# A decode-step backward kernel: the store of one 1280 KB weight-gradient block moved from Pool's DMA queue to ScalarE's, cut into 124 and 4 partitions

## The chip, the cores and the metric

One core of a Trainium2 chip. The metric is the device time of one execution in microseconds; the kernel before takes 739.5 us, the median of 3 runs (739.39 to 740.98).

## What is computed

The forward step and all gradients of a block that adds an attention with a KV cache and a gated MLP to its input, for one token:

```
xn  = layernorm(x)                                    # x: 1 x 640
q   = (xn @ wq)                                       # 32 heads of 128
p_h = softmax(q_h @ K_h^T / sqrt(128))                # K_h, V_h: 8192 x 128 for each head
o_h = p_h @ V_h
out = x + o @ wo + (silu(xn @ w1) * (xn @ w3)) @ w2
gradients of out, weighted with grad_out, by x, K, V, wq (640 x 4096), wo (4096 x 640), w1, w3, w2
```

All tensors are bfloat16. Nearly all of the bytes are K and V, which are read once, and dK and dV, which are written once: 2 MB each for every head. The gradient of wq is an outer product, dwq = xn^T dq, of 5 MB in all.

## The kernel before

The 32 heads run one after the other, in groups of four (`GH = 4`, `g` is the group), and everything is issued in an order that is written out by hand. For each head the four tiles of 128 partitions x 64 positions x 128 are handled like this: `product` multiplies K by q (V by grad_out @ wo^T) on VectorE and adds up over the 128 columns with matmuls by an identity; `probs`, `row_dots` and `dscores` make the softmax and its gradient; `outer` makes dV and dK, 48 of 64 rows on VectorE and 16 on ScalarE (L380, L387).

Transfers are in three queues:

- SP (`nc.sync`) loads K and V: V of head h+2 in the middle of head h (L115), K of head h+3 towards its end (L109). It also stores dV and dK of the last two heads, in halves (L392).
- Pool (`nc.gpsimd`) stores dV and dK of the other heads (L394), 2 MB each.
- ScalarE (`nc.scalar`) loads wo of the next group of heads at the second head of a group (L144) and stores the finished group's gradient of wo (L319). ScalarE takes these DMAs in its own order of instructions, between activations.

Weights of wq come in four blocks of eight heads (1024 columns, `GW = 8`), in two buffers `wq_0` and `wq_1` (`wq_bufs`). The gradient of a block is written over the block itself by ScalarE (L323, five activations for a group), in `finish_steps`, which is a generator: each `gap()` in the loop over the heads runs one step of it. For groups 0 to 5 the block's second group (odd `g`) starts the block's store. Blocks 0 and 1 go out from Pool column by column (L331, L396). Block 2, whose gradient is complete at head 24, and which is in a buffer that nothing loads again, goes into the list `late`; this list is given to Pool at head 29, behind the store of that head's dK (L126). Three stores are in it: wq's block 2 (1280 KB), wo of group 6 (640 KB) and wq of group 6 (640 KB).

`prep_steps(g)` makes q and the gradient of o for the next group. It needs wo of that group: `turn` transposes it on TensorE (L253), ScalarE copies it (L258), and L276 multiplies. TensorE works strictly in the order written, so what stands behind L253 waits with it: at head 26 that is the rest of this head's matmuls.

Of the kernel before, what the change touches and what calls it, by code (L numbers as in the profile page):

```python
# [16 lines left out]
P = 128  # L17
# [4 lines left out]
def kernel(  # L22
# [22 lines left out]
    nc = tc.nc  # L45
# [42 lines left out]
    dwq_v = out_4.rearrange("(p ci) n -> p ci n", ci=NC)  # L88
# [9 lines left out]
    with tc.manual_schedule(engines=ORDERED):  # L98
# [23 lines left out]
        def store(dst, src, later=False):  # L122
            if later:
                late.append((dst, src))
            else:
                nc.gpsimd.dma_start(dst, src)  # L126
# [164 lines left out]
        def on_cols(g):  # L291
            on = small.tile([P, GH], F32, name="on")
            nc.scalar.copy(on[:], grp[g]["on_ps"])
            on_bf = small.tile([P, GH], BF16, name="on_bf")
            nc.scalar.copy(on_bf[:], on[:])
            return on, on_bf
# [8 lines left out]
        def finish_steps(g):  # L305
            G_ = grp[g]
            wo_g = G_["wo"]
            on, on_bf = on_cols(g)
            behind_o.append((g, on_bf))
            yield  # L310
            assert not behind_o
            for r in range(GH):
                nc.scalar.activation(wo_g[:, r, :], g_bc_bf[:], ACTF.Copy, scale=on[:, r:r + 1])
                if r == 1:
                    yield
            if g == NG - 2:
                store(dwo_v[g], wo_g[:], True)
            else:
                nc.scalar.dma_start(dwo_v[g], wo_g[:])  # L319
            yield  # L320
            b, k = divmod(g, HB)
            for ci in range(NC):
                nc.scalar.activation(G_["wq"][:, ci, :], G_["dqbc"][:].rearrange("p h d -> p (h d)"),  # L323
                                     ACTF.Copy, scale=xn_col[:, ci:ci + 1])
            if g < NG - HB and k == HB - 1:
                cols = slice(b * GW * DH, (b + 1) * GW * DH)
                if g == NG - HB - 1:
                    store(dwq_v[:, :, cols], G_["wq_all"][:], True)
                else:
                    columns.extend((dwq_v[:, ci, cols], G_["wq_all"][:, ci, :]) for ci in range(NC))  # L330
                    nc.gpsimd.dma_start(*columns.pop(0))  # L331
            if g >= NG - HB:
                store(dwq_v[:, :, g * GH * DH:(g + 1) * GH * DH], G_["wq"], True)
            grp.pop(g)
# [148 lines left out]
        def keep_dq(st):  # L483
            G_, hh = st.G, st.hh
            if hh == 0:
                G_["dqbc"] = wpool.tile([P, GH, DH], BF16, name="dqbc_g", tag="dqbc_g", bufs=1)
            nc.scalar.copy(G_["dqbc"][:, hh, :], st.ps_db[:])
            if hh == GH - 1 and st.g < NG - 1:
                steps.append(finish_steps(st.g))
# [305 lines left out]
```

## Time and profile before

| | before |
|---|---|
| time, median of 3 runs | 739.5 us |
| the profiled execution: its own time / its span on the chip | 739.76 us / 737.9 us |
| busy: VectorE / TensorE / ScalarE / Pool | 85% / 76% / 63% / 7% of the span |
| DMA | 303.69 MB, mean 412 GB/s |
| DMA queue of SP / Pool / ScalarE | 155.41 MB / 139.42 MB / 7.87 MB |
| granted TensorE clock, mean | 0.774 |
| last VectorE instruction ends | 719.8 us |

Durations come from one profiled execution, and times inside it are counted from the start of its span. Its own time is 1.86 us more than the span, and 0.26 us more than the median of the runs. A DMA is worked on by 16 DMA engines at once, and its landing is the time at which the last of them is done. The line numbers are those of the kernel before; from L329 on the changed kernel's lines are one higher.

### The profile page before, as it was taken

The numbers are of one execution on the slowest core, as the hardware profiler recorded it, in microseconds if no ns is written. First come the engines' busy times: TensorE is split into PE (matmuls) and PEld (weight loads), VectorE is DVE, ScalarE is ACT, GpSimd is POOL, SyncE is SP. The second block draws the span as 40 slices with busy tenths as digits, with TensorE's granted clock in tenths as the row PEclk, the third lists the DMA queues.
The fourth block names the chain that finished last, engine by engine and source line by source line (L and its number), as shares of the span: only waits on it lengthen the run. The fifth ranks groups of instructions, "written<-read, shape, count | busy, mean of one in ns | idle before, by whom it ended". The sixth has DMA issues, their size and how long they took to land.

```text
span 737.9 us, 15773 instructions
## 1 busy us (share of the span) xinstructions
PE 560.1 (76%) x6498; PEld 326.3 (44%) x6513; DVE 628.8 (85%) x708; ACT 467.3 (63%) x1395; POOL 48.6 (7%) x93
## 2 busy tenths in 40 slices
PE   4768888786888788767788877787878767887860
PEld 3554445443544445434444434444444434454440
DVE  3689999997899989877998979699599988999990
ACT  2384566784678666674677656587377846777650
POOL 0010000000000110100000100100000000000100
PEclk9798779767777779667986788688678878867765
DMA  9998999999999999999999999999999999999992
GB/s 332 415 410 311 407 432 428 428 428 429 428 429 429 422 432 426 430 425 427 432 428 426 431 428 425 428 428 426 427 422 410 428 422 432 409 430 430 419 407 106
DMA packets 28389, 303.69 MB, mean 412 GB/s; under 512 B 3116, under 2 KB 4846, under 8 KB 10910
## 3 DMA queue, kind: packets, MB, share of 16 engines
q1 hardware_dynamic: 15202, 155.41, 50.6%
q0 software_dynamic: 11376, 139.42, 44.6%
q10 hardware_dynamic: 1740, 7.87, 2.6%
q8 instruction: 51, 0.84, 0.4%
q14 instruction: 20, 0.16, 0.1%
HBM read 151.34 MB, written 151.34 MB: 410 GB/s over the span
## 4 chain that ended last, share of the span: by engine, by line
DMA 60%; DVE 23%; PE 10%; ACT 3%; issue 1%; SPq 1%; DVEq 0%; ACTq 0%
DMA out_dram<-ot 33%; DMA Kt<-in_A_k_cache_dram 23%; DVE T L365 10%; DVE ot L387 8%; PE psS L367 3%; DMA out_dram<-wo_g 2%; DMA w3t<-in_B_w_dram 2%; ACT ot L380 2%; PE ob L451 1%; PE ob L429 1%; PE psDP L367 1%; DVE DP_sb L436 1%; SPq L158 1%; PE dx_ps L592 1%; DVE S_sb L402 1%
## 5 line engine op out<-in xcount | busy, mean ns | idle before, releaser
L367 PE MATMUL psDP<-T,ident_bf 128*128 128x512 bf16 x512 | 187.7, 533 | 58.0 <-DVE T L365 57.8
L367 PEld LDWEIGHTS <-ident_bf 128*128 128x128 bf16 x1024 | 123.8, 123 | 238.6 <-issue 191.1
L380 ACT ACTIVATE ot<-qs_g,Uf 128x128 bf16<-128x128 bf16 x496 | 151.5, 390 | 60.4 <-DMA out_dram<-ot 18.3
L365 DVE TENSOR_TENSOR T<-Kt,qs_g 128x4096 bf16<-128x4096 bf16 x64 | 146.4, 2289 | 30.6 <-DMA Kt<-in_A_k_cache_dram 29.1
L367 PE MATMUL psS<-T,ident_bf 128*128 128x512 bf16 x512 | 152.2, 451 | 21.6 <-DVE T L365 21.4
L380 ACT ACTIVATE ot<-do_g,Pf 128x128 bf16<-128x128 bf16 x504 | 154.0, 389 | 5.4 <-DMA out_dram<-ot 4.4
L365 DVE TENSOR_TENSOR T<-Vt,do_g 128x4096 bf16<-128x4096 bf16 x64 | 146.1, 2282 | 0.7 <-ACT do_g L284 0.6
L387 DVE TENSOR_TENSOR ot<-qs_g,U 128x3072 bf16<-128x3072 bf16 (+1 forms) x64 | 113.2, 1769 | 23.8 <-DMA out_dram<-ot 23.8
L387 DVE TENSOR_TENSOR ot<-do_g,P 128x3072 bf16<-128x3072 bf16 (+1 forms) x64 | 112.9, 1763 | 5.5 <-DMA out_dram<-ot 4.4
L394 POOL DMA_DIRECT2D out_dram<-ot x60 | 32.1, 535 | 583.0 <-DVE Uf L449 315.9
L451 PEld LDWEIGHTS <-Kt 128*128 128x128 bf16 x2048 | 57.7, 98 | 11.0 <-issue 8.2
L451 PE MATMUL ob<-U,Kt 128*128 128x1 bf16 x2048 | 57.1, 164 | 1.7 <-DVE U L444 1.5
L429 PEld LDWEIGHTS <-Vt 128*128 128x128 bf16 x2048 | 56.8, 98 | 0.0
L429 PE MATMUL ob<-P,Vt 128*128 128x1 bf16 x2048 | 56.1, 163 | 0.0
L423 ACT ACTIVATE Pf<-E,rZ 128x16 f32<-128x16 f32 x32 | 9.7, 305 | 59.8 <-DVE rZ L419 59.8
L470 ACT ACTIVATE dq_diag<-ident_bf,odq 128x128 bf16<-128x128 bf16 x32 | 12.8, 401 | 48.2 <-DVE odq L466 48.2
L406 PE MATMUL sm<-ident_f,mrow 128*128 128x128 f32 x64 | 18.6, 380 | 22.6 <-DVE mrow L404 22.4
L258 ACT COPY woT<-ps_t 128x512 bf16<-128x512 bf16 x40 | 23.0, 577 | 20.0 <-PE ps_t L253 20.0
L440 PE MATMUL sm<-rdot,ones_fc 128*128 128x1 f32 x64 | 11.3, 246 | 21.6 <-DVE junk L439 21.5
L253 PE MATMUL ps_t<-ident_bf,wo_g 128*128 128x128 bf16 x160 | 18.3, 247 | 10.2 <-ACT woT L258 6.7
L440 PEld LDWEIGHTS sm<-rdot,ones_fc 128*128 128x128 f32 x64 | 10.5, 191 | 34.3 <-DVE junk L439 32.2
L402 DVE TENSOR_REDUCE S_sb<-psS 128x64 f32<-128x512 f32 x32 | 21.9, 685 | 3.1 <-PE psS L367 3.1
(154 smaller groups left out, 501.6 us busy)
## 6 DMA issues: line engine op xcount, KB each, us to landing
out_dram<-ot POOLq DMA_DIRECT2D x60, 2048.0 KB, 30.5
Kt<-in_A_k_cache_dram SPq DMA_DIRECT2D x32, 2048.0 KB, 26.7
Vt<-in_A_v_cache_dram SPq DMA_DIRECT2D x32, 2048.0 KB, 21.5
out_dram<-ot SPq DMA_DIRECT2D x8, 1024.0 KB, 16.5
out_dram<-wo_g ACTq DMA_DIRECT2D x6, 640.0 KB, 15.5
wo_g<-in_A_wo_dram ACTq DMA_DIRECT2D x6, 640.0 KB, 15.8
wq<-in_A_wq_dram SPq DMA_DIRECT2D x2, 1280.0 KB, 27.8
out_dram<-wq POOLq DMA_DIRECT2D x10, 256.0 KB, 35.0
```

Source lines behind the costliest of these rows:

```text
L253: nc.tensor.transpose(ps_t[:, hh * DH:(hh + 1) * DH], wo_g[:, hh, ci * P:(ci + 1) * P], ident_bf[:])
L258: nc.scalar.copy(woT[:], ps_t[:])
L365: nc.vector.tensor_tensor(T[:], src[:, :, ds_], vec[:, ds_].unsqueeze(1).to_broadcast([P, J, DHH]), ALU.mult)
L367: nc.tensor.matmul(ps[:], lhsT=ident_bf[:], rhs=T[:, :, RUN * i:RUN * (i + 1)], start=(half == 0 and i == 0), stop=(half == 1 and i == DHH ...
L380: nc.scalar.activation(st.ot[:, j1 - ACT_J + j].rearrange("p a b -> p (a b)"), vec, ACTF.Copy, scale=wf[:, half, j:j + 1])
L387: nc.vector.tensor_tensor(st.ot[:, j0:j1], vec.rearrange("p (a b) -> p a b", b=2).unsqueeze(1).to_broadcast([P, n, DH // 2, 2]), w2[:, j0: ...
L394: nc.gpsimd.dma_start(dst[h], rows)
L402: nc.vector.tensor_reduce(st.S[:], st.ps["S"][:], AX.X, ALU.add)
L406: nc.tensor.matmul(st.sm[:, 8:8 + P], lhsT=mrow[:].to_broadcast([P, P]), rhs=ident_f[:], start=True, stop=True, skip_group_check=True)
L429: nc.tensor.matmul(st.ob[:, 0:1], lhsT=st.V[:, j, :], rhs=st.P2[:, j, 0:1], start=(j == 0), stop=(j == J - 1), skip_group_check=True)
L440: nc.tensor.matmul(st.sm[:, 4:5], lhsT=ones_f, rhs=rdot[:], start=True, stop=True, skip_group_check=True)
L451: nc.tensor.matmul(st.ob[:, 1:2], lhsT=st.K[:, j, :], rhs=st.U2[:, j, 0:1], start=(j == 0), stop=(j == J - 1), skip_group_check=True)
```

## The change

The store of wq's gradient block 2 (group 5 is the last before `NG - HB`, so `g == 5`, run in the last gap of head 24) no longer goes into `late`. ScalarE issues it at once, behind the activations that write the block, as two DMAs: one for partitions 0 to 123, one for partitions 124 to 127. The list `late` keeps the other two stores.

```diff
@@ finish_steps
             if g < NG - HB and k == HB - 1:
                 cols = slice(b * GW * DH, (b + 1) * GW * DH)
                 if g == NG - HB - 1:
-                    store(dwq_v[:, :, cols], G_["wq_all"][:], True)
+                    for p in (slice(0, 124), slice(124, P)):
+                        nc.scalar.dma_start(dwq_v[p, :, cols], G_["wq_all"][p])
                 else:
                     columns.extend((dwq_v[:, ci, cols], G_["wq_all"][:, ci, :]) for ci in range(NC))
                     nc.gpsimd.dma_start(*columns.pop(0))
```

Each partition holds five rows of 1024 columns (2048 bytes), which lie 8192 bytes apart in the output.

## The prediction

> **What bounds the kernel now.** First the page's second part, the span in 40 slices:
>
> ```profile
> DVE  3689999997899989877998979699599988999990
> DMA  9998999999999999999999999999999999999992
> GB/s 332 415 410 311 407 432 428 428 428 429 428 429 429 422 432 426 430 425 427 432 428 426 431 428 425 428 428 426 427 422 410 428 422 432 409 430 430 419 407 106
> ```
>
> All 16 DMA engines are busy from the second slice to the last but one, at some 428 GB/s. Only the last slice (18.4 us) is nearly empty, so I cut it into stretches of 2 us (start:end, length, five engines' busy times, clock, DMA share, GB/s):
>
> ```profile
> 722.00:724.00 2.00, 0.00 (x0) 0.00 (x0) 0.00 (x0) 0.00 (x0) 0.00 (x0) 0.50 0.82 299
> 724.00:726.00 2.00, 0.00 (x0) 0.00 (x0) 0.00 (x0) 0.00 (x0) 0.00 (x0) 0.50 0.15 51
> 726.00:728.00 2.00, 0.00 (x0) 0.00 (x0) 0.00 (x0) 0.00 (x0) 0.00 (x0) 0.50 0.07 27
> ...
> 732.00:734.00 2.00, 0.00 (x0) 0.00 (x0) 0.00 (x0) 0.00 (x0) 0.00 (x0) 0.50 0.06 25
> 734.00:736.00 2.00, 0.00 (x0) 0.00 (x0) 0.00 (x0) 0.00 (x0) 0.00 (x0) 0.50 0.05 21
> ```
>
> A share of 0.06 is one engine of 16. Fifteen engines are done at 724; one works on alone until 735.7, and the span ends 1.6 us after the last landing (736.3). So one engine, 12 us behind, sets the end. Third, the DMA issues (count, KB each, median us to landing):
>
> ```profile
> out_dram<-wo_g ACTq DMA_DIRECT2D x6, 640.0 KB, 15.5
> wo_g<-in_A_wo_dram ACTq DMA_DIRECT2D x6, 640.0 KB, 15.8
> ...
> out_dram<-wq POOLq DMA_DIRECT2D x1, 1280.0 KB, 34.7
> ```
>
> ScalarE's transfers are small, and still take 15 us. Last, the timelines of ScalarE (two rows) and TensorE around the place to which the store moves:
>
> ```profile
> 583.77 3.16 ACT L323 ACTIVATE wq<-dqbc_g,xn_col 128x512 bf16<-128x512 bf16 x5
> ...
> 597.82 0.34 ACTq L144 DMA_DIRECT2D wo_g<-in_A_wo_dram  x1
> ```
> ```profile
> 612.85 1.89 PE L367 MATMUL psS<-T,ident_bf 128*128 128x512 bf16 x8
> 614.57 0.39 PE L253 MATMUL ps_t<-ident_bf,wo_g 128*128 128x128 bf16 x4
> 614.80 1.75 PE L451 MATMUL ob<-U,Kt 128*128 128x1 bf16 x64
> ```
>
> The new store is issued at 586.9, behind L323. The next DMA of the same queue is wo's load, issued at 597.82; it lands at 612.94 (trace), and L253 needs it 1.6 us later. Behind L253 stands all of TensorE's work.
>
> **Removed.** Pool's store of 1280 KB at 685.42: 80 KB on each engine, 3.0 us at the last engine's 27 GB/s. It is queued work of the engine that sets the end, so alone this is worth -3.0 us. Pool's issue (0.85 us) has nothing waiting behind it.
>
> **Added: how many engines.** No DMA of 124 partitions is in the trace. By their packets, DMAs here are cut into equal shares: 128 partitions over 16 engines, 64 over 16, 5 (`fin_bf`) over 5, 1 (`x_row`) on one. Equal shares of 124 = 4 x 31 on at most 16 engines mean four; the bounds are 1 and 16. I take four: 155 rows of 2 KB each, and 5 more from the second DMA, 328 KB an engine. (The Trainium skill, DMA: Bandwidth & Descriptors, "Why a DMA increments its semaphore by 16 and not by 1", says the same: the largest number up to 16 that divides the slowest dimension, and the lowest-numbered engines.)
>
> **Added: is the last engine one of them?** In the tail the last engine's packets follow each other without a gap, and a 256-byte packet of `fin_bf` is one of them (723.6). So it is among the five that `fin_bf` uses. `x_row` (SP) and `g_row` (ScalarE), one packet each, ran on one and the same engine, so narrow DMAs seem to begin at the same place, and four of the five would be the new store's: 4 in 5 that it is. Then its bytes rise by 328 - 82 = 246 KB, 9.2 us; if not, they fall, -3.0 us.
>
> **Added: the queue.** 2 KB rows are in the trace, in wq's column loads (L137): packets of 84 ns, and of 768 such packets nearly all are followed on their engine by a packet of Pool's queue (16 KB, 611 ns). The queues take turns packet by packet, so with three queues full a 2 KB row costs a turn of 611 + 611 + 84 = 1306 ns. ScalarE's 640 KB DMAs confirm it: 8 packets an engine in 15.5 us. 160 rows would take 209 us, behind the store of wo (landed 597.8); by 614.6 only 13 have gone. wo's load stands behind the other 147 on these engines, so TensorE halts at L253. VectorE does some 8 us more (both halves of head 26's dK), then loads and stores stop too. The halt lasts until the slowest of the four has emptied. If it is the last engine, it has at 614.6, by the landings of before, 15 load packets and 35 store packets of 611 ns (the coming store included): 30.5 us. 35 rows go between them (2.9 us), the other 112 alone at 84 ns (9.4), then wo's 8 packets (1.6) and landing (1): the matmuls go on at 614.6 + 45.4 = 660.
>
> **What it costs.** VectorE's rows from 616 on hold 96 us of work; 8 are done in the halt, 88 are left, and VectorE runs without pause once nothing waits (as it does from 680 on): its end moves from 719.8 to 748. Most DMA engines end 4.5 us behind it (724.3 - 719.8 before): 752.5. By the engines' own work the sum is a little higher: they run dry at about 631 and stand until 662, 724 + 31 = 755. I take VectorE's figure, since loads run ahead once the engines are free. The last engine has caught up in the halt and falls back at before's rate (12 us in 724) by 1.5 us: 754. With 1.6 us to the span's end it is 755.6; with 1.86 around it 757.5, and 0.26 less for the median: **757 us**. The three us removed are inside, since the last engine no longer sets the end.
>
> **Two more waits** lie in the halt's cover. In the built program the load of K for head 30 (issued at 639.51 before) waits for the semaphore that the 124-partition store counts on; by 660 that store is through. And an issue itself can block: SP's third `w2c` load at 2.64 took 5.4 us, with some 107 descriptors an engine queued. The second new DMA stands behind 155, so ScalarE may stand at 587, and compute stop a head earlier; the same rows drain, so I leave the sum.
>
> **Rivals.**
> - *The last engine is the fifth, not one of the four.* The slowest of the four has 27 packets left (16.5 us) and lets through 18 rows (1.5), then 129 (10.8), 1.6 and 1: 646. VectorE ends at 734, and with 4.5, 1.5, 1.6 and 1.6 it is 743; the engines' own sum (dry 631 to 648) gives 746. Time 744. Against it: one in five; for it: nothing shows which of the five it is.
> - *All 16 engines share the rows*, 40 each: the store isn't confined. wo's load still waits 27 turns on the last engine, inside its 30.5 us: 649; VectorE ends at 737, time 747. Against it: 124 isn't divisible by 16.
> - *Many rows to a turn, last engine among the four.* If a turn takes some 13 rows, all 160 are through in 13 turns, by 614.6; wo's 8 packets need 8 turns of 1.42 us: 626. TensorE halts 11 us, which the queued 30 us of transfers cover, and the end is the last engine's +9.2: 748.7. The L137 packets, one to a turn, speak against it. (The Trainium skill, same page, "Queues, rings and completion order": an engine drains a whole packet, 9 to 17 descriptors typically, before it switches queues; by it the sum would be this rival's. The 768 packets here speak otherwise.)
> - *Faster: many rows to a turn, last engine not among the four.* The halt is covered as before, the last engine loses its 3.0 us, and the four, done by 724, get 9.2 more: 733. Time 736.5. It decides if wo's load lands before some 643, when the idle of the other engines reaches the 12 us by which the last one trails anyway.
>
> **How the numbers follow.** Forecast (757) 0.46; fifth engine (744) 0.18; all 16 (747) 0.06; many rows (748.7) 0.10; faster (736.5) 0.11; within 0.2%, where losses and the 3 us cancel, 0.05; beyond the forecast's range, if ScalarE's block adds to the halt, 0.04. A change of 0.2% (1.5 us) is about what can be told from none. Slower: 0.46 + 0.18 + 0.06 + 0.10 + 0.04 = 0.84. The range of 8 in 10 leaves out the faster case and what lies beyond: 739 to 768 (the forecast's own is 750 to 768, 768 with the halt 10 us longer).
>
> **What would show it.** After: ScalarE issues two stores near 587 and the first takes tens of us to land; wo's load lands near 640 to 660 instead of 613; TensorE waits at L253 for it; GB/s falls well under 400 in one or two slices between 630 and 665; VectorE ends near 748; the single-engine tail is much shorter than 12 us. Wrong, if wo's load lands within 20 us and L253 doesn't wait, or if the tail stays and only its length changes.

## The result, and the profile after

The changed kernel takes 744.85 us (median of 4 runs, 743.96 to 746.32), beside it the kernel before 740.05: a ratio of 1.0066, 95% interval 1.0045 to 1.0087. It is slower, as forecast, but by 4.8 us and not by 17.5. The profiled execution took 743.96 us with a span of 741.9 (before: 737.9).

The same rows of the page, 40 slices of 18.5 us:

```profile
DVE  4689899998899989877998978699699963999994
DMA  9998999999999999999999999999999987999996
GB/s 333 421 406 309 419 428 430 430 425 429 431 428 430 424 430 426 428 426 429 429 428 428 427 428 428 429 426 428 428 411 420 425 349 297 359 428 428 429 404 263
```

There is a dip, but it comes sooner than expected (three slices from 594 to 649, of 297 to 359 GB/s, where the forecast had one or two between 630 and 665); and the last slice moves 263 GB/s instead of 106. The tail in stretches of 2 us (the last two columns are the DMA share and GB/s):

```profile
730.00:732.00 2.00, 0.82 (x3) 0.52 (x3) 1.21 (x8) 0.65 (x2) 0.84 (x1) 0.50 1.00 412
732.00:734.00 2.00, 0.00 (x0) 0.00 (x0) 0.17 (x1) 0.00 (x0) 0.00 (x0) 0.50 0.94 364
734.00:736.00 2.00, 0.00 (x0) 0.00 (x0) 0.00 (x0) 0.00 (x0) 0.00 (x0) 0.50 0.86 297
736.00:738.00 2.00, 0.00 (x0) 0.00 (x0) 0.00 (x0) 0.00 (x0) 0.00 (x0) 0.50 0.11 35
738.00:740.00 2.00, 0.00 (x0) 0.00 (x0) 0.00 (x0) 0.00 (x0) 0.00 (x0) 0.50 0.00 0
```

The stretch with one engine at work (0.06 for 12 us) is gone: nearly all engines work until 736. VectorE works until 732.2, 12.4 us later than before. So the end is set by compute and the stores that follow it, no longer by one engine alone. Where the 12.4 us arise is in the timelines, ScalarE first, then TensorE and VectorE (start, duration, engine, line; in brackets the idle time before, and what ended it):

```profile
583.93 3.16 ACT L323 ACTIVATE wq<-dqbc_g,xn_col 128x512 bf16<-128x512 bf16 x5
587.12 24.88 ACTq L329 DMA_DIRECT2D out_dram<-wq  x2
612.04 0.31 ACT L424 ACTIVATE Pf<-E,rZ 128x16 f32<-128x16 f32 x1 [24.96 <-issue]
...
614.03 1.03 ACTq L144 DMA_DIRECT2D wo_g<-in_A_wo_dram  x1
```
```profile
622.96 0.58 PE L416 MATMUL sm<-rsum,ones_fc 128*128 128x1 f32 x2 [18.30 <-ACT E L415]
...
633.47 0.39 PE L253 MATMUL ps_t<-ident_bf,wo_g 128*128 128x128 bf16 x4
```
```profile
623.58 0.17 DVE L420 RECIPROCAL rZ<-sm 128x1 f32<-128x1 f32 x1 [16.00 <-PE sm L416]
```

ScalarE does nothing for 24.96 us but issue the two stores: 0.81 us for the first, 24.04 for the second. This is not a wait for a semaphore: the one that the second store counts on was last used by a load of K that had landed at 559.41. Behind the stand ScalarE has some 10 us of activations to make up for; the exponentials that it owes (L415) come at 622.5, TensorE waits 18.3 us for them, VectorE 16.0. VectorE's other pauses from 596 to its end are 5.2 us here and 8.9 before, so some 12.4 of the 16.0 us are left. L253, where the forecast put the halt, waits for nothing: wo's load is issued 16 us later than before, but it lands at 627.98, ahead of L253.

### The profile page after: what moved, and what is told of

It reads as the page before. It is cut to its first block, busy times and chain, and to the rows that moved or that the text cites. A ratio compares the mean times of both kernels' runs of the same rounds, so it can differ in the third digit from the quotient of the medians.

```text
span 741.9 us, 15786 instructions
## 1 busy us (share of the span) xinstructions
PE 556.0 (75%) x6513; PEld 322.4 (43%) x6513; DVE 628.7 (85%) x708; ACT 467.5 (63%) x1395; POOL 47.5 (6%) x92
## 4 chain that ended last, share of the span: by engine, by line
DMA 46%; DVE 29%; PE 13%; ACT 5%; ACTq 3%; issue 1%; SPq 1%; DVEq 0%
DMA Kt<-in_A_k_cache_dram 24%; DMA out_dram<-ot 19%; DVE T L366 14%; DVE ot L388 10%; PE psS L368 5%; ACTq L329 3%; ACT ot L381 3%; DMA wq<-in_A_wq_dram 2%; PE ob L430 2%; PE ob L452 1%; DVE DP_sb L437 1%; DVE S_sb L403 1%; PE dx_ps L593 1%; SPq L158 1%; PE psDP L368 1%
## 5 line engine op out<-in xcount | busy, mean ns | idle before, releaser
L368 PEld LDWEIGHTS <-ident_bf 128*128 128x128 bf16 x1024 | 122.2, 122 | 240.0 <-issue 189.3
L368 PE MATMUL psDP<-T,ident_bf 128*128 128x512 bf16 x512 | 181.0, 517 | 59.7 <-DVE T L366 59.6
L258 ACT COPY woT<-ps_t 128x512 bf16<-128x512 bf16 x40 | 23.0, 576 | 18.3 <-PE ps_t L253 18.3
L407 PE MATMUL sm<-ident_f,mrow 128*128 128x128 f32 x64 | 18.1, 371 | 20.6 <-DVE mrow L405 20.6
L416 PEld LDWEIGHTS sm<-rsum,ones_fc 128*128 128x128 f32 x64 | 16.2, 280 | 36.3 <-ACT E L415 32.8
L416 PE MATMUL sm<-rsum,ones_fc 128*128 128x1 f32 x64 | 13.8, 285 | 23.8 <-ACT E L415 23.8
```

The source lines that it names most:

```text
L258: nc.scalar.copy(woT[:], ps_t[:])
L368: nc.tensor.matmul(ps[:], lhsT=ident_bf[:], rhs=T[:, :, RUN * i:RUN * (i + 1)], start=(half == 0 and i == 0), stop=(half == 1 and i == DHH ...
L407: nc.tensor.matmul(st.sm[:, 8:8 + P], lhsT=mrow[:].to_broadcast([P, P]), rhs=ident_f[:], start=True, stop=True, skip_group_check=True)
L416: nc.tensor.matmul(st.sm[:, 3:4], lhsT=ones_f, rhs=rsum[:], start=True, stop=True, skip_group_check=True)
```

## The experiments

Three theories. *Issue*: the loss is ScalarE standing in the issue. *Queue*, the forecast's: wo's load stands behind the rows. *Imbalance*: the extra bytes of four engines. Each ratio is by five rounds beside the kernel before (740.84 us in the first four experiments, 740.05 in the next four, 740.48 in the last). The diffs show what stands in place of `store(dwq_v[:, :, cols], G_["wq_all"][:], True)` of the kernel before.

**1. The same stores behind wo's load.**

```diff
+ behind_wo.extend((dwq_v[p, :, cols], G_["wq_all"][p]) for p in (slice(0, 124), slice(124, P)))
...
  load_wo(g + 1, nc.scalar)
+ while behind_wo:
+     nc.scalar.dma_start(*behind_wo.pop(0))
```


> The same two stores of 124 and 4 partitions from ScalarE's queue, but issued behind wo's load (head 25, near 599 us) instead of ahead of it (587). Issue theory (the loss is ScalarE standing in the issue of 155 rows an engine until the queue has taken them): ScalarE stands some 25 us again, now from about 599, VectorE ends near 732 as in the changed kernel, time 743 to 747. Queue theory (the loss is wo's load behind the rows): wo's load lands near 613 as before, TensorE does not wait at L253, no halt, and only the four engines' 9.2 us are left: 737 to 742 if the last engine is not one of them or has slack, 749 if it is. Imbalance theory: 749 wherever the store stands.

Measured: 745.49 us, ratio 1.0064 (1.0049 to 1.0079), with no row ahead of wo's load. ScalarE:

```profile
598.54 0.34 ACTq L144 DMA_DIRECT2D wo_g<-in_A_wo_dram  x1
598.92 18.85 ACTq L685 DMA_DIRECT2D out_dram<-wq  x2
617.87 2.44 ACT L381 ACTIVATE ot<-qs_g,Uf 128x128 bf16<-128x128 bf16 x8 [24.94 <-issue]
```

VectorE waits 16.14 us and ends at 732.2. The queue and imbalance theories both miss; a stand, with wo's load out of the rows' way, is enough for the changed kernel's loss.

**2. Three of five columns, 93 rows an engine.**

```diff
+ for p, c in ((slice(0, 124), slice(0, 3)), (slice(124, P), slice(0, 3)), (slice(0, P), slice(3, NC))):
+     if p.stop == 124:
+         nc.scalar.dma_start(dwq_v[p, c, cols], G_["wq_all"][p, c])
+     else:
+         store(dwq_v[p, c, cols], G_["wq_all"][p, c], True)
```


> At head 24 ScalarE issues only three of the five columns for 124 partitions (93 rows on each of four engines); all the rest of the block goes out late from Pool as before. Issue theory: the queue takes 93 rows at once (SP's third w2c load stood only when some 107 descriptors an engine were queued), so ScalarE does not stand at 587; then the forecast's own wait must come: wo's load behind 93 rows of 1306 ns lands near 654 instead of 613, TensorE halts some 40 us at L253, and the time is about 750. If the issue stands here too, its length scales with the rows: some 15 us, time about 742. Imbalance theory (3/5 of 246 KB on the last engine, 5.5 us): 745.

Measured: 741.62 us, ratio 1.0010 (1.0001 to 1.0020). The store is taken at once, and the DMA behind it stands:

```profile
587.08 0.30 ACTq L330 DMA_DIRECT2D out_dram<-wq  x1
...
598.96 14.24 ACTq L144 DMA_DIRECT2D wo_g<-in_A_wo_dram  x1
```

So 93 rows and wo's 8 packets did not fit together. VectorE waits 10.81 us and ends at 727.8; the 750 us of a full halt did not come, because ScalarE's stand came first.

**3. The store late on Pool, cut 124 and 4.**

```diff
+ for p in (slice(0, 124), slice(124, P)):
+     store(dwq_v[p, :, cols], G_["wq_all"][p], True)
```


> The store stays where it was before (late, Pool's queue at head 29) and is only cut into 124 and 4 partitions. Imbalance theory, last engine one of the four: 246 KB more on it at 27 GB/s, +9.2 us: 749. Last engine not one of the four: its 82 KB are gone, -3.0 us, and the four others end 9.2 us later, at some 733, still ahead of it: 737. Issue and queue theories say nothing of Pool: they expect what the imbalance gives.

Measured: 749.95 us, +9.1, ratio 1.0116 (1.0101 to 1.0132), for 9.2 expected. VectorE ends at 720.4, 0.5 us later than before. The tail (last columns: share, GB/s) is longer by as much as the time:

```profile
728.00:730.00 2.00, 0.00 (x0) 0.00 (x0) 0.00 (x0) 0.00 (x0) 0.00 (x0) 0.50 0.35 145
...
736.00:738.00 2.00, 0.00 (x0) 0.00 (x0) 0.00 (x0) 0.00 (x0) 0.00 (x0) 0.50 0.13 53
...
742.00:744.00 2.00, 0.00 (x0) 0.00 (x0) 0.00 (x0) 0.00 (x0) 0.00 (x0) 0.50 0.09 34
```

0.35 is five to six engines, 0.13 two. By its time the last engine is one of the four that this store from Pool uses: otherwise, by the count above, the time would be 737. Whether ScalarE's store uses the same four, this run does not show.

**4. One store of 128 partitions at head 24 on ScalarE**, 40 rows on each of 16 engines.

```diff
+ nc.scalar.dma_start(dwq_v[:, :, cols], G_["wq_all"][:])
```


> At head 24 on ScalarE, but as one DMA of all 128 partitions: 40 rows on each of 16 engines. Issue theory: 40 rows are taken at once, ScalarE does not stand at 587. Queue theory of the forecast: wo's load behind 40 rows of 1306 ns lands near 640 to 650, TensorE halts some 30 us at L253, VectorE ends near 737, time 747. If neither a stand nor a halt shows, nothing is lost and the late 1280 KB are off every engine's end: 737.

Measured: 754.54 us, ratio 1.0184 (1.0170 to 1.0199), nearly three times the changed kernel's loss although no engine has more bytes than before. Nothing stands at the issue, and the forecast's wait is there:

```profile
588.06 0.64 ACTq L328 DMA_DIRECT2D out_dram<-wq  x1
...
598.70 0.36 ACTq L144 DMA_DIRECT2D wo_g<-in_A_wo_dram  x1
```
```profile
645.51 0.61 PE L253 MATMUL ps_t<-ident_bf,wo_g 128*128 128x128 bf16 x4 [29.69 <-DMA wo_g<-in_A_wo_dram]
```

VectorE waits 23.62 us and ends at 742.8. While loads and stores run beside them (597 to 624), the trace has 33 to 50 of these 2 KB packets in every 3 us on 16 engines: one per engine in 1.0 to 1.5 us, around the forecast's turn of 1.3. (The Trainium skill, DMA: Bandwidth & Descriptors, "Queues, rings and completion order", has an engine drain a packet of 9 to 17 descriptors typically before it switches; that would have put the 40 rows through in a few turns. The trace does not agree: they took from 596.8 to 638.1.)

**5. The changed kernel with its two stores in the other order.**

```diff
+ for p in (slice(124, P), slice(0, 124)):
+     nc.scalar.dma_start(dwq_v[p, :, cols], G_["wq_all"][p])
```


> The changed kernel with its two stores in the other order: 4 partitions first, then 124. Issue theory, as the runs so far refine it (a large DMA is taken at once, and it is the next one behind it that stands until about 100 rows an engine are left): neither store stands at 587, ScalarE works on until wo's load near 599 and stands there until some 613, as with 93 rows (14.2 us); VectorE ends near 728 instead of 732, time 742 to 745. If a DMA of 155 rows stands by itself, ScalarE stands at 587 for some 25 us in this order too, and the time is that of the changed kernel, 745.

Measured: 747.60 us, ratio 1.0095 (1.0080 to 1.0110), somewhat more than expected. The stand moves to the DMA behind the large one:

```profile
587.62 1.86 ACTq L329 DMA_DIRECT2D out_dram<-wq  x2
...
598.25 19.44 ACTq L144 DMA_DIRECT2D wo_g<-in_A_wo_dram  x1
```

A DMA of 155 rows an engine is taken in under 2 us; in the changed kernel it is the store of 4 partitions that stands. VectorE waits 16.04 us as there, but also 2.39 us more at 656.8, and ends at 735.5.

**6. Nothing issued on ScalarE behind the 155 rows.**

```diff
+ nc.scalar.dma_start(dwq_v[0:124, :, cols], G_["wq_all"][0:124])
+ store(dwq_v[124:P, :, cols], G_["wq_all"][124:P], True)
...
- load_wo(g + 1, nc.scalar)
+ load_wo(g + 1, nc.sync if g == NG - 2 else nc.scalar)
```


> The 124 partitions go out at head 24 from ScalarE, the other 4 late from Pool, and wo's load of the last group comes from SP: nothing is issued on ScalarE behind the 155 rows until the end. Issue theory: ScalarE does not stand, L253 does not wait. Then the rows take one turn each (1.3 us) and some 40 of 155 are gone at 640, where SP's load of K or V for head 30 waits for the store's semaphore: SP stops there, the queues run dry and the rest drains at 84 ns a row. If that wait decides: a halt of 20 to 40 us behind 640, 755 to 765. If the semaphore does not hold SP up: only the imbalance is left, 749 as with the late store cut in 124 and 4 (749.95).

Measured: 750.28 us, ratio 1.0129 (1.0111 to 1.0147). ScalarE does not stand, and a wait of the kind that the forecast named second takes its place. SP's waits between 600 and 700 (line, what it waited for, us in total, times, longest):

```profile
SPq L115 <- DMA out_dram<-wq: 43.6, 1, 43.6
```

SP issues nothing from 641.6 to 685.2, until the last row is out. The load that waits is V of head 30: with wo's load on SP too, the semaphores shift by one, and K of head 30, which shares the store's semaphore in the changed kernel, was issued at 641.20 without a wait. VectorE stands only from 681.4 to 695.6 (14.25 us), since it had loads ahead of it, and ends at 735.2. The time is nearly that of pure imbalance, but by the timeline it is this halt.

**7. As 4, with wo's load from SP** (its `load_wo` line as in 6).

```diff
+ nc.scalar.dma_start(dwq_v[:, :, cols], G_["wq_all"][:])
```


> The one store of 128 partitions at head 24 on ScalarE as in act_128 (754.5), but wo's load of the last group comes from SP, so that it is not behind the 40 rows. Queue theory for act_128: its whole 13.7 us are wo's load behind the rows, so with the load elsewhere TensorE does not wait at L253, VectorE ends near 720, and the time is that of before, 740 to 741 (the bytes of the last engine are the same). If the rows themselves slow the loads of K and V, some of the 13.7 us stay.

Measured: 740.04 us, ratio 1.0000 (0.9987 to 1.0012). One load taken out of the queue is worth the whole loss of experiment 4. VectorE still ends 4.7 us later than before (724.6); this costs nothing.

**8. Without the store.**

```diff
+ pass
```


> The store of wq's block 2 is left out altogether (that part of the output stays unwritten). The forecast's term for what is removed: 80 KB of the last engine at 27 GB/s, -3.0 us, 737.8 against a before of 740.8. If the end is not set by the last engine's bytes, less or nothing.

Measured: 737.55 us, -2.5, ratio 0.9960 (0.9948 to 0.9973), for -3.0 expected.

**9. Two of five columns, 62 rows an engine.**

```diff
+ nc.scalar.dma_start(dwq_v[0:124, 0:2, cols], G_["wq_all"][0:124, 0:2])
+ store(dwq_v[124:P, 0:2, cols], G_["wq_all"][124:P, 0:2], True)
+ store(dwq_v[:, 2:NC, cols], G_["wq_all"][:, 2:NC], True)
```


> At head 24 ScalarE issues two of the five columns for 124 partitions (62 rows on each of four engines); the rest of the block goes out late from Pool. Issue theory: 62 rows and wo's 8 packets are taken together, so ScalarE stands nowhere, compute goes on, and the forecast's wait comes in full: at 614.6 some 13 rows are gone, wo's load lands near 650, TensorE halts 30 to 36 us at L253, VectorE ends near 742 to 748 and the time is 752 to 760: fewer rows, and a longer time than with 93 (741.6) or 155 (744.9). If the cost follows the rows or the bytes on the four engines instead: 738 to 742.

Measured: 749.81 us, ratio 1.0118 (1.0104 to 1.0132): 62 rows cost 9.3 us, 93 rows 0.8, 155 rows 4.8. ScalarE's issues take 0.30 and 0.36 us, and TensorE shows the forecast's halt:

```profile
639.28 0.61 PE L253 MATMUL ps_t<-ident_bf,wo_g 128*128 128x128 bf16 x4 [23.63 <-DMA wo_g<-in_A_wo_dram]
```

The load took 40.4 us to land, 11 us less than the forecast's way of counting gives (near 650). The count of its first rival, in which the last engine isn't among the four, fits: 614.6, 27 packets (16.5 us), 18 rows between them (1.5), 31 alone (2.6), wo's packets (1.6) and landing (1) make 637.8; it landed at 639.23. VectorE waits 17.25 us and ends at 736.1.

**10. Four of five columns for all 128 partitions**, 32 rows on each of 16 engines: a wait with no imbalance.

```diff
+ nc.scalar.dma_start(dwq_v[:, 0:4, cols], G_["wq_all"][:, 0:4])
+ store(dwq_v[:, 4:NC, cols], G_["wq_all"][:, 4:NC], True)
```


> At head 24 ScalarE issues four of the five columns for all 128 partitions (32 rows on each of 16 engines, no engine has more than another); the fifth column goes out late from Pool. wo's load behind 32 rows of 1.2 us lands near 637, TensorE halts some 21 us, and VectorE stands about as long as in the changed kernel (16 us). If VectorE's end alone sets the time there: VectorE ends near 733 to 735 and the time is 744 to 748, as changed (744.9) though the engines are loaded alike. If part of the changed kernel's 4.8 us is the four engines' extra bytes: 740 to 743.

Measured: 750.53 us, ratio 1.0127 (1.0112 to 1.0143), above the range given: wo's load landed near 643, not 637, and VectorE waited 20.0 us, not 16, and ended at 740.4. The span ends 9.6 us behind that; in the changed kernel it is 9.7. Engines loaded alike or not, the end keeps the same distance from VectorE.

**11. The store early, on Pool.**

```diff
+ nc.gpsimd.dma_start(dwq_v[:, :, cols], G_["wq_all"][:])
```


> The store in one DMA of 128 partitions at head 24, but from Pool's queue, in its order between the stores of dV and dK. All theories: the bytes of the last engine are those of before, nothing is cut, no row is 2 KB by itself in ScalarE's queue; the stores behind it land some 6 us later (5 turns of 1.2 us), VectorE waits a little longer for a free tile, inside its 8 us of slack: 740 to 741. Slower by more would mean that an early store costs by its place alone.

Measured: 742.26 us, ratio 1.0023 (1.0013 to 1.0033). VectorE waits 8.62 us at 637.9 for a tile whose store is late, and ends 7.4 us later than before, of which 1.8 reach the time. An early place costs a little by itself.

**12. Late on Pool, cut 120 and 8.**

```diff
+ for p in (slice(0, 120), slice(120, P)):
+     store(dwq_v[p, :, cols], G_["wq_all"][p], True)
```


> The store stays late on Pool and is cut into 120 and 8 partitions instead of 124 and 4. By equal shares on at most 16 engines, 120 go to 15 engines (40 rows each) and 8 to 8 (5 rows each), one engine gets nothing. If that one is the last engine: -3.0 us, 737. If the last engine is one of the eight: 45 rows for 40, +0.4 us, 740.5 to 741; if among the other seven, no change.

Measured: 742.18 us, ratio 1.0019 (1.0006 to 1.0031). A gain of 3 us is excluded: 15 engines do not leave out the last one. The +1.7 is more than the 0.4 for five more rows; what the rest is stays open. None of the kernels beats the one before, save that which leaves a store out.

## Why the prediction was right and wrong

Set against VectorE's end, the spans of these kernels look like this:

| kernel | VectorE ends | span | difference |
|---|---|---|---|
| before | 719.8 | 737.9 | 18.1 |
| store left out | 720.5 | 735.5 | 15.0 |
| late, 124 and 4 | 720.4 | 745.9 | 25.5 |
| late, 120 and 8 | 721.0 | 740.9 | 19.9 |
| 128 partitions, wo from SP | 724.6 | 738.5 | 13.9 |
| early on Pool | 727.3 | 740.0 | 12.7 |
| 93 rows | 727.8 | 739.7 | 11.9 |
| **changed** | 732.2 | 741.9 | 9.7 |
| behind wo's load | 732.2 | 743.6 | 11.4 |
| wo from SP, 4 late | 735.2 | 746.1 | 10.9 |
| 4 first, then 124 | 735.5 | 745.5 | 10.0 |
| 62 rows | 736.1 | 747.5 | 11.4 |
| 128 partitions, 4 columns | 740.4 | 750.0 | 9.6 |
| 128 partitions | 742.8 | 753.6 | 10.8 |

Where VectorE ends at 727.8 or later, the span follows it by 9.6 to 11.9 us, whatever the four engines were given. Where it ends earlier, the span goes with the last engine's bytes, wherever VectorE ends: 737.9 to 740.9 with some 80 KB of this store on it, 735.5 without, 745.9 with 246 KB more. The kernel before has some 8 us of room between the two, and the change moves from one group to the other: 12.4 us of VectorE, less the 8.4 us by which the difference shrinks, are the 4.0 us of the span.

- *The bound* was right: with compute left alone, 246 KB more on the last engine cost 9.1 us for 9.2, and 82 KB less gain 2.5 for 3.0 (experiments 3 and 8).
- *Four engines*: right. (The Trainium skill, DMA: Bandwidth & Descriptors, "Why a DMA increments its semaphore by 16 and not by 1", takes the largest number up to 16 that divides the slowest dimension, here four. The trace agrees: both new stores have four landings by the engines.)
- *The last engine among the four*: wrong, and this is one of the two steps that failed. The last engine shows by its landings. Before the change, the store that Pool issued at 603.93 has 15 landings by 624.95 and the last at 637.69. In the changed kernel, the store that Pool issued at 581.48 has 15 by 602.77 and the last at 615.72; the K load issued at 595.71 has 15 by 609.71 and the last at 618.17. Between 609.8 and 615.7 the trace has, beside the 2 KB rows, only 16 KB packets of 611 ns, one right behind the other, from the queues of SP and Pool in turn: one engine, working off what was queued for these two last landings, with no row among them. So the last engine got none of the rows: by the prediction's reading of `fin_bf` it is the fifth of the five, and its bytes fell by 80 KB instead of rising by 246. In the forecast's halt, 14 us rested on it (660 against the 646 of the rival without it). Experiments 2 and 5 agree: wo's load has five late landings there, four of them 1.5 to 1.6 us behind the four of the store, and the fifth apart. Experiment 3 put the last engine among its four, but from Pool's queue.
- *One row to a turn*: right; 1.0 to 1.5 us for a row while loads and stores run (experiment 4).
- *wo's load waits behind the rows and halts TensorE at L253*: a real mechanism, seen in experiments 4, 9 and 10 (7 takes it out of 4 and the loss is gone), but not what happens in the changed kernel. Where it happens, the forecast's price for it is too low: VectorE ends 97 us after TensorE goes on (645.5 to 742.8 in experiment 4), not 88. It starts 3.0 us behind TensorE, has 89.9 us of work left and pauses for 4.4.
- *The other step that failed*, and the one that changes the path, is the last sentence on the two waits: "ScalarE may stand at 587, and compute stop a head earlier; the same rows drain, so I leave the sum". ScalarE does stand, and this replaces the halt. Compute stops with ScalarE, so new loads and stores stop being queued at once. In the trace 15 to 22 rows go out in 3 us until 606, and 124 to 148 from 609 to 618, when they have the four engines to themselves. And the stand does not last until the last row is out: it ends with on average 87 rows an engine still to go (271 of 620 were out at 612.0). The halt would have lasted until all rows and wo's packets were through; the last row went out at 624.1, where the forecast had TensorE go on at 660.
- In the sum, that is *the term for VectorE's end*: +28.2 forecast (719.8 to 748), +12.4 measured. The forecast's 7.6 us from VectorE's end to the span's end were 9.7. (From the last landing to the span's end it was 4.0 us instead of 1.6; see the last section.) So -15.8 and +2.1, and with them the forecast of 757.5 for this execution becomes 743.8; it took 743.96.
- *A load behind the store's semaphore*: real where the stand is absent (experiment 6, 43.6 us, for V of head 30 instead of K), and rightly hidden in the changed kernel, where the store was through by 625.
- The rival of 16 engines, at 747, is experiment 4: right in kind, 7.5 us too low.
- The rival of the fifth engine, at 744, has the right engine, and the measured 744.85 beside it. The nearness is luck: its halt at L253 until 646 did not come, and at the 97 us of experiments 4, 9 and 10 it would have cost some 9 us more.

That the last engine no longer trails at the end fits: it had 3.0 us less to do, and it worked on while the others had run dry. Of the store that Pool issued at 632.05 its share landed at 648.78, 1.6 us behind the others, where it had been 12.7 before. Open: why this engine trails at all, and what sets the number of rows at which the next DMA stands.

## What to carry to other kernels

A DMA issued from a compute engine's queue costs more than its bytes. Before moving one there, ask three things of the trace: how many packets it puts on each engine (here 128 partitions went to 16 engines, 124 = 4 x 31 to four), what is queued behind it, and whether the next DMA of that queue finds room or makes the engine stand. And find both ends of the kernel, compute's and the DMA engines': a loss on the one that has room shows only from where the room is used up.

## What was not expected of the hardware

- A queue takes one DMA of 155 rows an engine in under 2 us, but the next one, even of 5 rows, stands until some rows are out. On average of the four engines 75 to 106 rows were left when ScalarE went on (93 rows: 75; the changed kernel: 87; small store first: 89; behind wo's load: 106). 62 rows and wo's 8 packets made nothing stand, nor did 40 and 8.
- Less can cost more: 62 rows cost 9.3 us and 93 cost 0.8, because the stand that 93 rows cause keeps the longer wait from arising.
- The program ends with an instruction of Pool, at the kernel's closing line, that begins when Pool issues its last DMA and ends 3.9 to 4.2 us behind the last packet of Pool's queue (13 of the 14 kernels; 1.0 us in experiment 3). Before the change and in the changed kernel (count, then the shortest, median and longest in ns):

```profile
L790 POOLq DRAIN  x3: 40/102/18507, 718.6 to 737.6; - x3
L791 POOLq DRAIN  x3: 40/102/10231, 730.9 to 741.7; - x3
```

  In the changed kernel it ends at 741.2, 3.3 us behind the last landing of any DMA (737.9), and the span ends 0.8 us later; before, it ended at 737.1, 0.8 us behind the last landing. So where compute ends late, Pool's closing instruction sets the end, and not the last landing. That it waits for Pool's queue is read from the constant distance alone, and whether another queue for Pool's last store would save those 3 us was not tried.
